# Reordering the small steps around a fused MLP stage: factors, weight halves, row loads and low parts moved

## The chip, the cores and the metric

The kernel runs on one core of a Trainium2 chip. The core has five instruction streams that matter here: PE (matrix products, 128x128), DVE (elementwise and reductions, reads PSUM), ACT (elementwise with a function table, reads PSUM), POOL (elementwise, SBUF only) and SP, which in this kernel only issues DMA transfers. Each stream executes in its own program order; streams wait for each other through semaphores. The metric is the device time of one execution in microseconds (us), the median of several runs.

## The reference

The input x is a sequence of 2048 rows of 448 numbers, in float32. Two branches and a skip are added:

```python
xn = layernorm(x)                       # eps 1e-5, no scale or shift
q = xn @ wq                             # 16 heads of 28
k, v = xn @ wk, xn @ wv                 # one shared key and value head of 28
o = softmax(q k^T * 28**-0.5) v         # per head, over all 2048 keys
y = layernorm(xn)                       # the second norm of the MLP branch
h = gelu(y @ w1 + b1)                   # 448 -> 1792, tanh form
out = x + o @ wo + (h @ w2 + b2)        # 1792 -> 448
```

## The kernel before, in words

Rows are handled in four chunks of 512 (`NCH`, 4 tiles of 128 each, `CT`). There is no planner: `tc.manual_schedule()` keeps the order in which the Python code emits instructions, engine by engine, and the framework only adds the waits. So a step that stands earlier in the code stands earlier on its engine, and an engine whose next instruction waits holds everything behind it. All DMA of this part goes through SP's queue, in code order.

Products are made in three parts for accuracy: a value is split into a rounded high part and a low part (the rest), and high*high, low*high and high*low are accumulated.

Stage 1, the projections (about the first 66 us). For each chunk c and each of four column groups i, `q_slot` emits eleven products into one PSUM bank. The eviction of a group (`evac`) is emitted one slot later: for chunks 2 and 3 DVE multiplies the bank by a row of factors (L388), ACT rounds it to the high part (L389), and `low()` lets DVE subtract for the low part (L396) and issues the stores of both parts to DRAM (`qd`, L403) and, for group 0, the key rows (`ks`, L399). Between these, `w1_split` cuts the first MLP weight into parts (ACT L353, POOL L354, L355), and a dictionary `more` places small jobs at slots by `later(c, i, job)`. Among those jobs are the norm factors. `bn_end` turns means and variances into the factors of the first norm by `rstd` (DVE L200, ACT square root L202, DVE L203 to L206, and the shift, L246). Chunk 0 needs a second set of factors for the second norm; it is made in two generators of two tiles each, at slots (2,2) and (2,3), followed by a Tanh on one element that makes ACT load the table used from then on (L448).

Stage 2, the MLP (about 66 to 471 us). It is a row of 56 slots, `slot(n)`, one for each chunk and each 128-wide block of the 1792 hidden columns, in the chunk order 2, 3, 0, 1, plus two more to drain. A slot n emits `mlp1`, the eleven products of block n, then two ACT reads of the bank (hx L643, hz L644) and two POOL steps (L645, L646); then it emits `mlp2` of block n-2, twelve products (L673) of the finished hidden block with `w2` into four banks. In between, by a table `stages` whose key is the product's number, stand: `texp` (two exponentials L613 and, behind the second, four stores of 256 KB to DRAM, `td`, L616), `closing` (ACT rounds the previous block, hh L656; POOL makes its low part, hl L658) and `middle` (ACT tanh L649, POOL L650, L651). A block therefore passes hx, hz, L645, L646, tanh, L650, L651, hh, hl before its `mlp2` two slots later. The second weight is cut two blocks at a time by `w2_split`: `high` on ACT (L367), `low` half on DVE and half on POOL (L371), then the load of a further pair (L359). In the first slots of chunk 2 there is a special order, `n == 1` and `n == 2`. The memory of `w2h` and `w2l` is that of the projections' tiles, so their first writes wait for the last stores of the projections.

Two other jobs fill each slot, one step behind every few products: `mxs`, the row maximum of query-key products for the softmax (PE L561, DVE L562), of which 784 are spread over the MLP and attention stages, and `tq`, whole rows of scores of some heads kept transposed later (PE L595, DVE L596 into `raw`, two buffers, a buffer being free again when its `td` stores have landed). Both take PSUM banks `m` from a ring of three.

For each chunk's result the rows of x are loaded again (`line`, L271, 224 KB each, tile `a` with four buffers) from block 10 on, and POOL adds b2 one block later (L728, L731). The last `mlp2` of a chunk adds the bank to them (DVE L678) and stores them (`ad`, L679). At block 8 of the last chunk `load_q(0)` clears a tile on POOL (L524) and issues four query loads on SP (L530).

Stage 3, attention (about 471 us to the end), is not touched. It takes as many of the `mxs` steps in each of its steps as its weights give it of those that are left, so that what the MLP stage does not do is done there.

Of the kernel before, what the change touches and what calls it, by code (L numbers as in the profile page):

```python
# [16 lines left out]
P = 128  # L17
# [24 lines left out]
def block_kernel(ctx, tc, x, wq, wk, wv, wo, w1, b1, w2, b2, out):  # L42
# [150 lines left out]

    def rstd(dst, var, n, norms):
        m = len(norms)
        v = tmp.tile([P, 3, m, n], F32, name=f"rs{m}{n}", bufs=2)
        s, r, w = (v[:, i] for i in range(3))
        for i, second in enumerate(norms):
            by, plus = (1.0 + EPS, EPS * EPS) if second else (1.0, EPS)
            dve.tensor_scalar(s[:, i], var, by, plus, op0=ALU.mult, op1=ALU.add)  # L200
        yield s
        act.activation(r, s, AF.Sqrt)  # L202
        dve.reciprocal(r, r)  # L203
        dve.scalar_tensor_tensor(w, r, -0.5, r, op0=ALU.mult, op1=ALU.mult)
        dve.tensor_mul(w, w, s)
        dve.scalar_tensor_tensor(dst, w, 1.5, r, op0=ALU.add, op1=ALU.mult)  # L206
        yield
# [9 lines left out]
    def bn_end(c, k0=0, n=CT):  # L217
        for k in range(k0, k0 + n):
            dve.bn_aggr(lnp[:, CT * c + k, :], sts[c][:, k, :])
        ts = slice(CT * c + k0, CT * c + k0 + n)  # L220
        norms = (False, True) if c else (False,)
        r = rstd(lnrq[:, 0:len(norms), ts], lnp[:, ts, 1], n, norms)
        at = next(r)
        yield
        next(r)
        shift(c in KEPT, ts)
        yield
        if c in KEPT:
            ratio = ratios[c] = tmp.tile([P, CT], F32, name="ratio", bufs=2)
            dve.tensor_mul(ratio, at[:, 1], lnq[:, ts])  # L230
            dve.tensor_mul(ratio, ratio, lnr[:, ts])
        elif c:
            shift(True, ts)
        else:
            r = rstd(lnrq[:, 1:2, ts], lnp[:, ts, 1], n, (True,))
            next(r)
            yield
            next(r)
            shift(True, ts)
        yield  # L240

    ratios = {}
# [14 lines left out]
    def stats(c):  # L257
        for k in range(CT):
            bn(CT * c + k)
        g = bn_end(c)  # L260
        next(g)
        next(g)
        return g
# [38 lines left out]

    def norm_first(bank):
        center, turn = norm_parts(0, False, True, bank)
        ends = seconds
        bn(0)
        bn(1)
        next(ends[0])
        next(ends[0])
        bn(2)  # L310
        bn(3)
        next(ends[1])
        center(0)
        center(1)
        next(ends[1])
        spin(21)
        turn(0)
        spin(2)
        turn(1)
        center(2)  # L320
        center(3)
        spin(8)
        turn(2)
        spin(1)
        turn(3)
        next(first)
# [98 lines left out]
            pe.matmul(idle if t is None else t, ident, ident, start=True, stop=True)  # L425

    idle = mtile([P, P])
    seconds = [bn_end(0, 0, 2), bn_end(0, 2, 2)]
    norm_first(qbank)
    seconds.append(stats(1))  # L430
    more = {}

    def later(c, i, job, ahead=False):
# [2 lines left out]
    for c, at in ((2, ((0, 1), (0, 2), (0, 2), (0, 3))), (3, ((1, 0), (1, 1), (1, 2), (1, 3)))):  # L436
# [4 lines left out]
            later(c - 1, 0, lambda g=g: next(g), True)  # L441
        later(c - 1, 1, lambda g=g: next(g))
        later(c - 1 if c == 2 else c, 3 if c == 2 else 0, lambda c=c: unscale(c), c == 3)
    for g, at in zip((seconds[0], seconds[1], seconds[2]), ((2, 2), (2, 2), (1, 0))):
        later(*at, lambda g=g: next(g))
    for g in seconds[0:2]:
        later(2, 3, lambda g=g: next(g))
    later(2, 3, lambda: act.activation(warm, one, AF.Tanh))  # L448

    def b1_turn():  # L450
        pb = mtile([P, NF])
# [25 lines left out]
    for c in range(NCH):  # L477
        if c + 1 < NCH:
            center, turn = norm_parts(c + 1, False, bank=lambda shape: (qbank, mtile)[next(turns) % 2](shape))
        for i in range(4):  # L480
            ev = q_slot(c, i)
            if vt is not None:
                v_slot(c, vt)
                vt = None
            low = None
            if evac is not None:
                vt, low = evac()
            evac = ev
            if i in ((2, 3) if c == 0 else (1, 3)):
                n = 2 * c + i // 3  # L490
                w1_split(n)
                if n < 2:
                    w1_load(n + 4)
                elif n == 3:
                    w1_load2(6)
                elif n in (4, 5):
                    w2_load(n - 4)
                if n in (2, 3):
                    qms.append(load_m(*heads[n - 2]))
                elif n in (4, 5):  # L500
                    load_m(TURNED[n - 4], 3, q3[n - 4])
            for job in more.get((c, i, True), ()):
                job()
            for part, k in (("", "c0 c1", "t0 c2 t1 c3", "t2 t3") if c == 0 else
                            ("c0 c1", "t0 c2 t1 c3", "t2 t3", "") if c + 1 < NCH else [""] * 4)[i].split():
                if part == "t" and low is not None:
                    low()
                    low = None
                (center if part == "c" else turn)(int(k))
            if low is not None:  # L510
                low()
            for job in more.get((c, i, False), ()):
                job()
    evac()[1]()
    for c in KEPT:
        xts[c, True] = xts.pop((c, False))
    ph1a.close()
# [115 lines left out]
    def split(c, ft):  # L633
        return c == 0 and ft % 2 == 1

    def mlp1(c, ft):
        yh, yl = xts[MLP_ORDER[c], True]
        ph = m2p.tile([P, CW], F32, name="m2_3") if (c, ft) == (0, 1) else php.tile([P, CW], F32, name="ph")
        fs = slice(ft * P, (ft + 1) * P)
        yield from proj_steps(ph, lambda b: w1h[:, b, fs], lambda b: w1l[:, b, fs], yh, yl)  # L640
        hx = hrp.tile([P, CW], F32, name="hx", bufs=2)
        hz = hrp.tile([P, CW], F32, name="hz", bufs=2)
        act.activation(hx, ph, AF.Identity, bias=b1t[:, ft:ft + 1])  # L643
        act.activation(hz, ph, AF.Square, bias=b1s[:, ft:ft + 1], scale=GELU[0] ** 0.5)  # L644
        pool.tensor_scalar(hz, hz, 1.0, 1.0, op0=ALU.mult, op1=ALU.add)  # L645
        pool.tensor_mul(hz, hz, hx)  # L646

        def middle():
            act.activation(hz, hz, AF.Tanh, scale=GELU[1])  # L649
            pool.tensor_scalar(hz, hz, 0.5, 0.5, op0=ALU.mult, op1=ALU.add)  # L650
            pool.tensor_mul(hx, hx, hz)  # L651

        def ending():
            hh = hrp.tile([P, CW], F32R, name="hh")
            hl = hrp.tile([P, CW], F32R, name="hl")
            act.activation(hh, hx, AF.Copy)  # L656
            hs[c, ft] = (hh, hl)
            pool.tensor_sub(hl, hx, f(hh))  # L658

        return middle, ending  # L660

    def mlp2(c, ft, stages):
        if ft == 0:
            m2s[c] = [m2p.tile([P, CW], F32, name=f"m2_{k}")[:, 0:D] for k in range(CT)]
        m2 = m2s[c]
        hh, hl = hs.pop((c, ft))
        terms = ((hh, w2h), (hh, w2l), (hl, w2h))
        order = [(k, i) for k in range(CT) for i in range(3)]
        if (c, ft) == (0, 0):
            order.sort(key=lambda e: e[1])  # L670
        for n, (k, i) in enumerate(order):
            h, w = terms[i]
            pe.matmul(m2[k], h[:, k * P:(k + 1) * P], w[:, ft, :], start=(ft == 0 and i == 0),  # L673
                      stop=(ft == NF - 1 and i == 2))
            if ft == NF - 1 and i == 2:
                t = CT * MLP_ORDER[c] + k
                a = lines.pop(t)
                dve.tensor_add(a, a, m2[k])  # L678
                nc.sync.dma_start(ad[:, t, :], a)  # L679
            stages[n]()  # L680
            yield

    def slot(n):
# [1 line left out]
        middle = high = low = none  # L685
        closing, ending = ending, none
        if n < len(mslots):
            if split(*mslots[n]):
                high, low = w2_split(n // 2)
                if n > 1:  # L690
                    high()
            middle, ending = yield from mlp1(*mslots[n])
        if n == 2:
            for _ in range(3):
                maxed += mxs.step()
            later_low()
        texp = turned_exp if n < len(mslots) - 1 else none
        stages = {0: texp, 1: texp, 2: low, 3: closing, 5: middle}
        if n == 1:
            stages, later_low = {0: closing, 1: high, 5: middle}, low  # L700
        if n in norms:
            stages = {4: norms[n], 5: texp, 6: texp, 7: closing, 8: norms[n], 9: middle, 10: low}
        if n >= 2:
# [16 lines left out]
    for n in range(len(mslots) + 2):  # L720
        c, ft = mslots[n] if n < len(mslots) else (NCH, n - len(mslots))
        if 3 <= ft < 11 and ft % 2 and len(KEPT) <= c + 1 < NCH:
            line(CT * MLP_ORDER[c + 1] + (ft - 3) // 2)
        if 9 < ft:
            line(CT * MLP_ORDER[c] + ft - 10)
            if ft > 10:
                a = lines[CT * MLP_ORDER[c] + ft - 11]
                pool.tensor_add(a, a, b2b)  # L728
        if ft == 0 and n:
            a = lines[CT * MLP_ORDER[c - 1] + CT - 1]  # L730
            pool.tensor_add(a, a, b2b)  # L731
        if (c, ft) == (NCH - 1, 8):
# [281 lines left out]
```

## Time and profile before

| what | value |
|---|---|
| median of three runs | 1086.64 us (1086.4 to 1087.1) |
| the profiled execution | 1086.84 us |
| its span, first to last instruction | 1085.1 us |
| around the span | 1.7 us |
| granted clock of PE | 0.999 |
| PE busy | 1072.9 us, 5889 products |
| DVE, ACT, POOL busy | 907.4, 726.8, 562.0 us |

A row of the timeline has: start in us from the span's beginning, length, engine, line of the kernel, operation, output<-inputs, shape, and in brackets how long that engine had been idle before it and what ended the idle time. SPq is SP issuing DMA. Rows of equal instructions are merged (x4). A row of the windows has: the stretch, its length, busy us and instruction count of PE, PEld (weight loads), DVE, ACT, POOL, then the granted clock, the mean busy share of the DMA engines and their GB/s. The product instructions overlap by about half, so starts, not lengths, tell PE's pace.

### The profile page before, as it was taken

Reading aid. Unit: us, or ns where it says so; the run is one execution under the profiler, and the core shown is the slowest. Engines: PE = TensorE matmul, PEld = TensorE weight load, DVE = VectorE, ACT = ScalarE, POOL = GpSimd, SP = SyncE. Lnnn points to the kernel's source line nnn. Section 1 sums busy time; section 2 is a strip of 40 time slices with the busy share of each in tenths; the row PEclk is TensorE's granted clock in tenths of the full one; section 3 lists DMA queues with packets and bytes.
Section 4 is the critical chain, followed back from the end, with each engine's and each line's share of the span. In section 5 each row is a group of like instructions: output and inputs, shape, how many; then the busy total and the mean of one; then the engine's idle time right before and its main releaser. Section 6 shows DMA issues by size and latency. Waiting matters only on the chain.

```text
span 1085.1 us, 17677 instructions
## 1 busy us (share of the span) xinstructions
PE 1072.9 (99%) x5889; PEld 721.6 (67%) x5889; DVE 907.4 (84%) x1846; ACT 726.8 (67%) x1262; POOL 562.0 (52%) x694
## 2 busy tenths in 40 slices
PE   9989999999999999999999999999999999999998
PEld 8768888888888888865555556555556555555455
DVE  6789899898988998877999997899997889886744
ACT  6665556666666666559777776677775777765784
POOL 5359897778777877854333433433442343243220
PEclk9999999999999999999999999999999999999999
DMA  8774456777877777776977798588796778885820
GB/s 268 251 213 140 121 142 170 195 179 179 214 187 180 184 196 192 210 163 152 201 187 185 179 219 206 145 196 190 184 212 172 177 174 199 201 200 131 186 53 34
DMA packets 140102, 194.45 MB, mean 179 GB/s; under 512 B 17078, under 2 KB 95596, under 8 KB 140012
## 3 DMA queue, kind: packets, MB, share of 16 engines
q1 hardware_dynamic: 127276, 171.43, 62.8%
q0 software_dynamic: 11328, 21.33, 8.5%
q8 instruction: 46, 0.75, 0.3%
q10 hardware_dynamic: 1408, 0.57, 0.2%
q14 instruction: 44, 0.36, 0.1%
HBM read 114.30 MB, written 77.71 MB: 177 GB/s over the span
## 4 chain that ended last, share of the span: by engine, by line
PE 90%; DMA 4%; DVE 3%; issue 1%; POOL 1%; ACT 1%; SPq 0%; DVEq 0%; POOLq 0%; ACTq 0%
PE po L903 21%; PE m L561 18%; PE m L931 17%; PE m L673 12%; PE ph L182 10%; PE m L595 5%; DMA raw<-in_B_w_dram 1%; PE m L793 1%; PE m L794 1%; PE m L795 1%; PE ph L185 1%; PE ph L187 1%; PE po L886 1%; PE m L886 1%; DMA a<-in_A_x_dram 1%
## 5 line engine op out<-in xcount | busy, mean ns | idle before, releaser
L562 DVE TENSOR_REDUCE mx<-m 128x1 f32<-128x512 f32 x784 | 506.5, 679 | 78.2 <-PE m L561 68.4
L932 ACT ACTIVATE p<-m 128x512 f32<-128x512 f32 x784 | 402.6, 609 | 161.4 <-PE m L931 161.2
L561 PE MATMUL m<-ks,qm 128*128 128x512 f32 x784 | 321.4, 410 | 0.7 <-DVE mx L562 0.6
L931 PE MATMUL m<-xh,ks 128*128 128x512 f32 x784 | 257.3, 397 | 0.1
L903 PE MATMUL po<-p,vs 128*32 128x512 f32 x1920 | 230.8, 598 | 0.0
L561 PEld LDWEIGHTS m<-ks,qm 128*128 128x128 f32 x784 | 147.0, 187 | 116.8 <-ACT p L932 37.0
L596 DVE TENSOR_SCALAR_CACHE_REDUCE raw<-m 128x512 f32<-128x512 f32 x240 | 161.6, 689 | 17.4 <-PE m L595 10.6
L931 PEld LDWEIGHTS m<-xh,ks 128*128 128x128 f32 x784 | 146.1, 188 | 42.1 <-issue 5.8
L914 DVE STREAM_TRANSPOSE p<-half 128x1024 f32<-128x1024 f32 x120 | 148.2, 1236 | 5.3 <-PE m L886 2.0
L613 ACT ACTIVATE raw<-raw,m 128x1024 f32<-128x1024 f32 x120 | 133.0, 1150 | 2.0 <-DVE m L602 2.0
L903 PEld LDWEIGHTS po<-p,vs 128*32 128x32 f32 x1920 | 50.1, 109 | 113.4 <-issue 108.4
L643 ACT ACTIVATE hx<-ph,b1t 128x512 f32<-128x512 f32 x55 | 37.9, 690 | 124.2 <-PE ph L187 120.2
L595 PE MATMUL m<-ks,q 128*128 128x512 f32 x240 | 94.6, 394 | 1.7 <-DVE raw L596 1.7
L658 POOL TENSOR_TENSOR hl<-hx,hh 128x512 fp32r<-128x512 f32 x56 | 72.5, 1295 | 33.2 <-ACT hh L656 33.2
L673 PE MATMUL m<-w2h,hl 128*128 128x448 f32 x224 | 82.1, 368 | 1.4 <-POOL hl L658 1.4
L673 PE MATMUL m<-w2l,hh 128*128 128x448 f32 x224 | 81.4, 365 | 0.6 <-DVE w2l L371 0.6
L673 PE MATMUL m<-w2h,hh 128*128 128x448 f32 x224 | 81.3, 364 | 0.2 <-DMA td<-raw 0.2
L646 POOL TENSOR_TENSOR hz<-hz,hx 128x512 f32<-128x512 f32 x56 | 72.8, 1300 | 4.7
L548 POOL DMA_DIRECT2D xh<-mn x15 | 8.2, 545 | 129.2 <-ACT mn L544 129.2
L651 POOL TENSOR_TENSOR hx<-hx,hz 128x512 f32<-128x512 f32 x56 | 72.4, 1293 | 4.7
L182 PE MATMUL ph<-xh,w1h 128*128 128x512 f32 x165 | 65.0, 394 | 0.0
L182 PE MATMUL ph<-xh,w1l 128*128 128x512 f32 x165 | 64.5, 391 | 0.0
(182 smaller groups left out, 1384.0 us busy)
## 6 DMA issues: line engine op xcount, KB each, us to landing
td<-raw SPq DMA_DIRECT2D x240, 256.0 KB
half<-td SPq DMA_DIRECT2D x120, 512.0 KB
xh<-qd POOLq DMA_DIRECT2D x60, 168.0 KB, 4.2
a<-in_A_x_dram SPq DMA_DIRECT2D x28, 224.0 KB
qm<-qd POOLq DMA_DIRECT2D x112, 56.0 KB, 4.2
qd<-qe SPq DMA_DIRECT2D x24, 256.0 KB
qm<-qd SPq DMA_DIRECT2D x84, 56.0 KB
ad<-a SPq DMA_DIRECT2D x16, 224.0 KB
```

The costliest lines, as they stand in the source:

```text
L182: pe.matmul(ps, w, v, start=(n == 0), stop=False)
L561: pe.matmul(pm, qm[:, t * P:(t + 1) * P], ks[:, n * CW:(n + 1) * CW], start=True, stop=True)
L562: dve.tensor_reduce(mx[:, CT * j + t, n:n + 1], pm, axis=AX.X, op=ALU.max)
L595: pe.matmul(sc, q3[i][:, t * P:(t + 1) * P], ks[:, n * CW:(n + 1) * CW], start=True, stop=True)
L596: dve.tensor_scalar(raw[:, :, 4 * n:4 * n + 4, :].rearrange("p r b i -> p b r i"), sc.rearrange("p (b r i) -> p b r i", r=4, i=32), SCALE, ...
L613: act.activation(raw[:, rs], raw[:, rs], AF.Exp, bias=m3[:, 4:5], scale=1.0)
L646: pool.tensor_mul(hz, hz, hx)
L673: pe.matmul(m2[k], h[:, k * P:(k + 1) * P], w[:, ft, :], start=(ft == 0 and i == 0), stop=(ft == NF - 1 and i == 2))
L903: pe.matmul(po[32 * j:32 * j + 32, :], vs[:, kt, :], ps.pop((u, kt, j)), start=(kt == 0), stop=(kt == NT - 1))
L914: dve.transpose(p.rearrange("p k (g j) -> p g k j", j=32), halves[u, kt // 8][:, :, 32 * (kt % 8):32 * (kt % 8) + 64].rearrange("p g (k j) ...
L931: pe.matmul(s, ks[:, kt * P:(kt + 1) * P], qss[u][:, j, :], start=True, stop=True)
L932: act.activation(p, s, AF.Exp, scale=SCALE)
```

## The change

The four parts of the change are these.

1. The second factors of chunk 0 are made for all four tiles in one generator, `second_of_first`, at slots (3,0) and (3,1), and the Tanh that loads the table follows at (3,1). `rstd` keeps one buffer instead of two where it works on four tiles; `ratio` has three instead of two.
2. In slot (3,3) of the projections the eviction of (3,3), its product with the factors and its rounding, is emitted at once, ahead of the low part of (3,2).
3. In the first three MLP slots: `w2_split(0)` and its `high` stand at the end of slot 0, its `low` in slot 1; `middle` stands earlier in slots 0 and 1; three `mxs` steps that slot 2 took ahead of its `mlp2` are left out there.
4. In the last chunk the rows of x are loaded at blocks 5 to 8 and b2 added at blocks 6 to 9. In the last slot `closing` of block 12 stands ahead of the two ACT reads of block 13. In the very last `mlp2` the twelve products go by pairs of banks: hh with w2h for both, hh with w2l for both, then hl with w2h for both.

```diff
     def rstd(dst, var, n, norms):
-        v = tmp.tile([P, 3, m, n], F32, name=f"rs{m}{n}", bufs=2)
+        v = tmp.tile([P, 3, m, n], F32, name=f"rs{m}{n}", bufs=2 if n < CT else 1)
...
-        else:
-            r = rstd(lnrq[:, 1:2, ts], lnp[:, ts, 1], n, (True,))
-            next(r)
-            yield
-            next(r)
-            shift(True, ts)
+        yield
+
+    def second_of_first():
+        ts = slice(0, CT)
+        r = rstd(lnrq[:, 1:2, ts], lnp[:, ts, 1], CT, (True,))
+        next(r)
+        yield
+        next(r)
+        shift(True, ts)
         yield
...
-    for g, at in zip((seconds[0], seconds[1], seconds[2]), ((2, 2), (2, 2), (1, 0))):
-        later(*at, lambda g=g: next(g))
-    for g in seconds[0:2]:
-        later(2, 3, lambda g=g: next(g))
-    later(2, 3, lambda: act.activation(warm, one, AF.Tanh))
+    later(1, 0, later_one)
+    g = second_of_first()
+    for k in (0, 1):
+        later(3, k, lambda g=g: next(g))
+    later(3, 1, lambda: act.activation(warm, one, AF.Tanh))
...
                 (center if part == "c" else turn)(int(k))
+            if (c, i) == (NCH - 1, 3):
+                _, end = evac()
             if low is not None:
                 low()
...
-    evac()[1]()
+    end()
...
     def mlp1(c, ft, before):
...
+        before()
         act.activation(hx, ph, AF.Identity, bias=b1t[:, ft:ft + 1])
...
             order.sort(key=lambda e: e[1])
+        if (c, ft) == (NCH - 1, NF - 1):
+            order.sort(key=lambda e: (e[0] // 2, e[1]))
...
-            if split(*mslots[n]):
+            if split(*mslots[n]) and n > 1:
                 high, low = w2_split(n // 2)
-                if n > 1:
-                    high()
-            middle, ending = yield from mlp1(*mslots[n])
-        if n == 2:
-            for _ in range(3):
-                maxed += mxs.step()
-            later_low()
+                high()
+            before = none
+            if n == len(mslots) - 1:
+                before, closing = closing, none
+            middle, ending = yield from mlp1(*mslots[n], before)
         texp = turned_exp if n < len(mslots) - 1 else none
         stages = {0: texp, 1: texp, 2: low, 3: closing, 5: middle}
+        if n == 0:
+            high, later_low = w2_split(0)
+            stages = {0: texp, 1: middle, 2: texp, 3: high}
         if n == 1:
-            stages, later_low = {0: closing, 1: high, 5: middle}, low
+            stages = {0: closing, 1: later_low, 2: middle}
...
-        if 9 < ft:
-            line(CT * MLP_ORDER[c] + ft - 10)
-            if ft > 10:
-                a = lines[CT * MLP_ORDER[c] + ft - 11]
-                pool.tensor_add(a, a, b2b)
-        if ft == 0 and n:
+        k = ft - (10 if c < NCH - 1 else 5)
+        if c < NCH and 0 <= k < CT:
+            line(CT * MLP_ORDER[c] + k)
+        if c < NCH and 0 < k <= CT:
+            a = lines[CT * MLP_ORDER[c] + k - 1]
+            pool.tensor_add(a, a, b2b)
+        if ft == 0 and 0 < c < NCH:
```

More of the change, by code (lines that the diff above doesn't have):

```diff
@@ L228, in bn_end @@
         if c in KEPT:
-            ratio = ratios[c] = tmp.tile([P, CT], F32, name="ratio", bufs=2)
+            ratio = ratios[c] = tmp.tile([P, CT], F32, name="ratio", bufs=3)
             dve.tensor_mul(ratio, at[:, 1], lnq[:, ts])
@@ L304, in norm_first @@
         center, turn = norm_parts(0, False, True, bank)
-        ends = seconds
+        ends = [bn_end(0, 0, 2), bn_end(0, 2, 2)]
         bn(0)
@@ L427, in block_kernel @@
     idle = mtile([P, P])
-    seconds = [bn_end(0, 0, 2), bn_end(0, 2, 2)]
     norm_first(qbank)
-    seconds.append(stats(1))
+    g = stats(1)
+    later_one = lambda g=g: next(g)
     more = {}
@@ L634, in split, with mlp1 @@
         return c == 0 and ft % 2 == 1
-    def mlp1(c, ft):
+    def mlp1(c, ft, before):
         yh, yl = xts[MLP_ORDER[c], True]
```

## The prediction

> **What bounds the kernel now.** I read first the busy shares, then the groups of instructions with their idle time, then the windows, and last the timeline of PE around the places that the change touches. The two rows below are of the page: the share of PE, and what the last products of a hidden block wait for.
>
> ```profile
> PE 1072.9 (99%) x5889; PEld 721.6 (67%) x5889; DVE 907.4 (84%) x1846; ACT 726.8 (67%) x1262; POOL 562.0 (52%) x694
> L673 PE MATMUL m<-w2h,hl 128*128 128x448 f32 x224 | 82.1, 368 | 1.4 <-POOL hl L658 1.4
> ```
>
> The windows show (PE, PEld, DVE, ACT, POOL, then clock, DMA share, GB/s) that the clock is full and that nothing is left to gain in the attention stage:
>
> ```profile
> 480.00:1060.00 580.00, 580.00 (x3480) 310.50 (x3473) 477.03 (x875) 419.42 (x810) 209.27 (x336) 1.00 0.76 178
> ```
>
> PE is the bound throughout: 580.00 of 580 us there, 1072.9 in all. The number of products stays what it was, so only an idle gap of PE can be closed or opened. Those within reach of the change are in the timeline (the bracket is PE's idle time and who ended it):
>
> ```profile
> 62.47 0.43 PE L410 MATMUL m<-ident,vt 32*128 32x32 f32 x4 [0.69 <-ACT vt L393]
> 70.11 0.50 PE L595 MATMUL m<-ks,q 128*128 128x512 f32 x1 [1.33 <-DVE raw L596]
> ...
> 78.53 0.44 PE L673 MATMUL m<-w2h,hh 128*128 128x448 f32 x1 [0.23 <-DMA td<-raw]
> 80.67 0.67 PE L673 MATMUL m<-w2l,hh 128*128 128x448 f32 x2 [0.61 <-DVE w2l L371]
> 87.11 0.37 PE L673 MATMUL m<-w2h,hl 128*128 128x448 f32 x1
> ...
> 436.86 0.50 PE L595 MATMUL m<-ks,q 128*128 128x512 f32 x1 [0.40 <-DVE raw L596]
> 463.77 0.47 PE L673 MATMUL m<-w2h,hl 128*128 128x448 f32 x1 [0.74 <-POOL hl L658]
> 468.09 0.47 PE L673 MATMUL m<-w2h,hl 128*128 128x448 f32 x1 [0.69 <-POOL hl L658]
> 472.13 0.50 PE L561 MATMUL m<-ks,qm 128*128 128x512 f32 x1 [0.58 <-DVE mx L562]
> ```
>
> Early 0.69+1.33+0.23+0.61 = 2.86, in the last MLP chunk 0.40, at its end 0.74+0.69+0.58 = 2.01: 5.27 us, 0.49% of the time. That is all that the change could win. The sum is made against the profiled execution (1086.84 us, span 1085.1 and 1.7 around it), 0.20 above the median of 1086.64.
>
> **Part 1 and 2, the projections' end.** DVE and POOL at slot (2,3), then ACT and DVE at the end of (3,3):
>
> ```profile
> 55.43 1.44 DVE L204 SCALAR_TENSOR_TENSOR rs<-rs 128x2 f32<-128x2 f32 x1
> 57.09 0.52 DVE L206 SCALAR_TENSOR_TENSOR lnrq<-rs 128x2 f32<-128x2 f32 x1
> 58.58 0.69 DVE L388 TENSOR_TENSOR qp<-qp,ib 128x512 f32<-128x512 f32 x1
> ...
> 55.24 1.61 POOL L354 TENSOR_TENSOR w1l<-raw,w1h 128x672 fp32r<-128x672 f32 x1 [6.24 <-issue]
> 55.31 1.28 ACT L448 ACT_TABLE_LOAD   x1
> 66.62 0.94 ACT L353 ACTIVATE w1h<-pair 128x896 fp32r<-128x896 f32 x1
> 68.14 0.60 ACT L389 ACTIVATE qe<-qp 128x512 fp32r<-128x512 f32 x1 [0.57 <-ACT w1h L353]
> 67.36 0.69 DVE L388 TENSOR_TENSOR qp<-qp,ib 128x512 f32<-128x512 f32 x1
> 69.37 0.68 DVE L596 TENSOR_SCALAR_CACHE_REDUCE raw<-m 128x512 f32<-128x512 f32 x1
> ```
>
> The factor chain is eleven small DVE steps from 55.2 to 58.6. Two of them (1.44 and 0.52, where their likes in the second chain take 0.16) lie beside POOL's L354: DVE is held. So the bank of (2,3), at 58.58, is multiplied some 3.4 us after its turn. The change takes both chains out here: that multiply comes at about 54.8, and the 0.69 at 62.47 goes (its vt is a job of ACT that stood behind the late banks). One chain of six steps comes back at (3,0) and (3,1), behind another w1 split. POOL's steps of that split stand beside it again, so I charge it the same 1.44+0.52+3x0.16 = 2.4, and the table load of 1.28 falls on ACT before a rounding. One square root fewer on ACT costs less than 0.3 and hides beside PE. The last multiply (67.36) comes to about 65.7: the low part of (3,2) no longer stands ahead of it, 0.7 from the order, and 1.0 from the gap closed before. ACT then does the last split (66.62 moves little) and the rounding at 67.1 to 67.6 rather than 68.14. DVE's last low part ends, and the first raw eviction starts, at about 68.4 rather than 69.37. The fourth L595 stands at 69.1 rather than 70.11: **a lead of 1.0 us**. Bounds: none of it, if the rounding stays behind the split and the chain is held for longer; 1.33, the whole gap.
>
> **Part 3, w2 and the first slots.** Does the lead reach mlp2? Rows of SP, the windows of 72 to 75, DVE, PE and POOL:
>
> ```profile
> 66.54 4.68 SPq L403 DMA_DIRECT2D qd<-qe  x8
> ...
> 72.00:73.00 1.00, 1.00 (x6) 0.79 (x5) 1.00 (x3) 0.88 (x1) 0.26 (x1) 1.00 1.01 369
> 73.00:74.00 1.00, 1.00 (x6) 0.84 (x5) 1.00 (x3) 1.00 (x2) 0.00 (x0) 1.00 0.21 72
> 74.00:75.00 1.00, 1.00 (x6) 0.84 (x5) 1.00 (x2) 1.00 (x3) 0.08 (x1) 1.00 0.00 0
> ...
> 74.56 0.69 DVE L596 TENSOR_SCALAR_CACHE_REDUCE raw<-m 128x512 f32<-128x512 f32 x1
> 79.65 0.96 DVE L371 TENSOR_TENSOR w2l<-raw,w2h 128x448 fp32r<-128x448 f32 x1
> 70.92 0.40 PE L561 MATMUL m<-ks,qm 128*128 128x512 f32 x1
> 71.16 0.39 PE L182 MATMUL m<-xh,w1l 128*128 128x512 f32 x1
> ...
> 76.88:86.82 9.94, 9.10 (x40) 7.09 (x39) 9.40 (x18) 7.44 (x10) 9.69 (x11) 1.00 0.34 82
> ```
>
> w2's memory is free when the last query stores have landed. DMA is full until 73 and empty from 74, so the first high half can start at about 74.2. It takes 0.94 (its like is 66.62). Put at the end of slot 0 it stands on ACT ahead of hx(1) and hz(1), and DVE's low half (0.96) ahead of the four raw evictions that began at 74.56. So these begin at 75.1+0.96 = 76.1, and the fourth L595 waits for a bank; I charge 0.4 us of new idle. The gaps of 0.23 and 0.61 at 78.53 and 80.67 have their cause removed. The first mlp2 starts at about 77.7 rather than 78.53, but 3 x 0.24 = 0.7 us of that (an L561 to the next product, 70.92 to 71.16) is the three products that now run in the attention stage, where PE has no gap to take them.
>
> The next gate is POOL. The last window is from the start of L645(1) to the end of hl(1): POOL is busy 9.69 of 9.94 us, so hl(1) comes when that row of steps is through. L645(1) needs hx(1) and hz(1), which stand behind the high half: 74.2+0.94, then two reads of some 0.7 each, so it begins at about 76.5 rather than 76.88, and 9.6 us later hl(1) ends at about 86.1 rather than 86.82. PE uses hl(1) at 87.11 before and at about 86.06 after: 1.05 gained, less 0.7 = **0.35**. Parts 1 to 3 together win 0.4. SP: the next w2 load goes out a slot sooner, into DMA that is empty at 74 to 75, at no cost; if it met the stores of `td` instead, they would land later by its share. Bounds: if part 3 only stalls, 0.9 lost; if both gaps close and the lead stays, 1.0 gained.
>
> **Part 4a, the rows of the last chunk.** POOL and SP around block 8, and the gap that follows:
>
> ```profile
> 423.28 1.81 POOL L524 MEMSET xh<- 128x2048 f32 x1
> 425.11 1.65 SPq L530 DMA_DIRECT2D xh<-qd  x4
> 426.87 3.58 SPq L616 DMA_DIRECT2D td<-raw  x4
> 429.00:430.00 1.00, 1.00 (x6) 0.81 (x6) 0.99 (x3) 0.00 (x0) 0.92 (x1) 1.00 0.99 213
> 435.00:436.00 1.00, 1.00 (x6) 0.83 (x5) 0.00 (x0) 0.00 (x0) 1.00 (x2) 1.00 0.54 172
> 436.10 0.69 DVE L596 TENSOR_SCALAR_CACHE_REDUCE raw<-m 128x512 f32<-128x512 f32 x1 [1.87 <-PE m L595]
> 459.23 1.15 POOL L728 TENSOR_TENSOR a<-a,b2b 128x448 f32<-128x448 f32 x1
> ```
>
> Four loads and four adds move; three of the four adds fall on idle POOL. The add of block 8 takes 1.15 and now stands right before the memset of 423.28. SP's four query loads wait for the memset (425.11 = 423.28+1.81), and behind them in SP's order stand the four `td` stores of 426.87. DVE's eviction at 436.10 is ready 1.87 us before it runs, DMA being 0.99 busy at 429: it waits for those stores to free a `raw` buffer, and PE's 0.40 at 436.86 is what is left of that wait. So the add goes through whole: memset 424.4, loads 426.3, stores 428.0, eviction 437.25, PE idle 0.40+1.15 = 1.55. **Loss 1.15.** Bounds: a gain of 0.40, if the store's issue isn't what the eviction waits for; a loss of 2.3 if a row load also stands in front (a rival, below). I take the add alone, as the memset and the issues follow each other without a gap.
>
> **Part 4b, the end of the MLP.** POOL and PE:
>
> ```profile
> 462.43 1.29 POOL L658 TENSOR_TENSOR hl<-hx,hh 128x512 fp32r<-128x512 f32 x1
> 466.77 1.27 POOL L658 TENSOR_TENSOR hl<-hx,hh 128x512 fp32r<-128x512 f32 x1
> 471.16 0.40 PE L931 MATMUL m<-xh,ks 128*128 128x512 f32 x1
> ```
>
> `closing` of block 12 comes two ACT reads sooner: hl(12) ends at about 461.3 rather than 463.72, and the 0.74 at 463.77 goes. POOL's chain of block 13 starts behind it and ends at the same 468.02, so what PE gains there it waits at hh(13) and hl(13). By pairs of banks, eight L673 and three L561 are left behind hl(13), where there were ten and four: the 3.07 us from 468.09 to 471.16 for fourteen products become 3.07x11/14 = 2.4, and the attention's L931 starts at 470.5. The last adds on DVE move with it, and so does the 0.58 at 472.13. **Gain 0.6.** Bounds: 0, if the last three adds crowd DVE and the maximum comes later; 1.4, if the 0.69 at 468.09 shrinks as well.
>
> **Sum:** 1086.84 - 0.4 + 1.15 - 0.6 = 1087.0, and 0.2 less for the median: 1086.8 us.
>
> **The rivals.** (A) Faster: the wait at 436.10 is a wait for transfers in flight, not for their issue, so the add costs nothing; and parts 1 to 3 keep all of the lead and both w2 gaps: 1.0+0.23+0.61+0.11. With 0.6 to 1.1 at the end this is 2.5 to 3.0, hence about 1084. For it speaks that DMA is only 0.54 busy just before the eviction; against it, that DVE is then idle and a store whose issue is late lands late.
>
> (B) Slower in 4a: SP's row load of slot 50 is issued ahead of the query loads and the stores. Its 224 KB at the 213 GB/s of the window at 429 are 1.1 us more, so the gap grows to 2.65 and the time is 1087.9. The window's share of 0.99 speaks for it; against it, that the load can go out while SP waits for the memset. The Trainium skill, page "DMA: Bandwidth & Descriptors", section "Queues, rings and completion order", has a rule for it: on each DMA engine descriptors are consumed in the order of the ring, so what is issued first is read first. By that rule the row load is always in front, and the sum would be 1087.9 rather than 1086.8; no row here shows the order within a ring.
>
> (C) The other side, clearly slower: the new place of w2's first high half turns the landing of the last query store into a gate for everything. ACT waits with hx(1) behind it, DVE with the four evictions behind w2's low half. Each us that the landing is past 74.2 then costs one. It decides from 76.2, where 2 us are lost and the end is 1089. For it: the last eight stores are issued only from 66.54 to 71.2. Against it: DMA carries 72 GB/s at 73 and nothing at 74.
>
> (D) The change moves gaps and closes none: the three products cost 0.7 and give 0.7, hl(13) is as late as before, and the time is 1086.6.
>
> **How the numbers follow.** My forecast has a chance of 0.50, A 0.16, B 0.17, C 0.12, D 0.05. About 0.2% (2.2 us) is what a measurement of this kernel can tell from no change. Faster by more than that (below 1084.5) is most of A: 0.15. Slower by more (above 1088.8) is C and a part of B where further loads add up: 0.17. Within it is the rest, 0.68. Range: from 1084.4, A's value with a little lost, to 1089.0, C's point of decision. The likeliest case alone, by its bounds, reaches from 1085.2 to 1088.2.
>
> **What would show it.** Part 1: the multiply of (2,3) at 55 rather than 58.58, no idle at 62.47, the idle before the fourth L595 about as long but 1 us sooner. Part 3: w2's first high half on ACT at 74 to 75, hl(1) ending by 86.1. Part 4a: POOL's memset at 424.4 and PE idle for 1.5 at the eviction after block 8; if it stays under 0.5 the step is wrong. Part 4b: the idle of 0.74 gone and L931 at 0.6 sooner against the gap before it. Most of all a chain of small DVE steps in chunk 3 held longer than 2.4 us would make the prediction wrong, or a POOL step that is late for another reason.

## The result and the profile after

The changed kernel takes 1088.51 us (median of 11 runs, 1087.24 to 1090.46) beside 1086.78 for the kernel before on the same chip (1085.93 to 1087.67): 1.0019 of it, 95% interval 1.0011 to 1.0027. It is slower by 1.7 us, where 0.2 was forecast; the time lies in the range, and the cause was not the one in the sum. A second series of the same kernel (below) gave 1088.13. The mean granted clock is 0.997 or 0.998 in six of the eleven executions, which are the six longest (1088.51 to 1090.46), and 0.999 or 1.000 in the other five (1087.24 to 1088.44).

Lines below 200 are the same in both kernels; behind that the changed kernel's are 3 to 10 higher (L595 is now L600, L596 L601, L561 L566, L673 L681, L371 L374, L367 L370, L651 L657 and L645 L651). The timeline of the changed kernel, PE's longer idle times first, then ACT, DVE and POOL:

```profile
70.16 0.47 PE L600 MATMUL m<-ks,q 128*128 128x512 f32 x1 [2.56 <-DMA ks<-qe]
78.71 0.50 PE L600 MATMUL m<-ks,q 128*128 128x512 f32 x1 [0.32 <-DVE raw L601]
88.17 0.47 PE L681 MATMUL m<-w2h,hl 128*128 128x448 f32 x1 [0.65 <-POOL hl L664]
438.60 0.50 PE L600 MATMUL m<-ks,q 128*128 128x512 f32 x1 [1.29 <-DVE raw L601]
468.45 0.47 PE L681 MATMUL m<-w2h,hh 128*128 128x448 f32 x1 [0.72 <-ACT hh L662]
1046.54 0.42 PE L896 MATMUL m<-p,vs 128*32 128x256 f32 x4 [0.58 <-ACT p L942]
...
76.38 0.95 ACT L370 ACTIVATE w2h<-raw 128x896 fp32r<-128x896 f32 x1 [2.07 <-DMA qd<-qe]
54.35 0.69 DVE L391 TENSOR_TENSOR qp<-qp,ib 128x512 f32<-128x512 f32 x1
59.65 1.40 DVE L204 SCALAR_TENSOR_TENSOR rs<-rs 128x4 f32<-128x4 f32 x1
61.28 0.51 DVE L206 SCALAR_TENSOR_TENSOR lnrq<-rs 128x4 f32<-128x4 f32 x1
424.12 1.16 POOL L738 TENSOR_TENSOR a<-a,b2b 128x448 f32<-128x448 f32 x1
425.22 1.81 POOL L529 MEMSET xh<- 128x2048 f32 x1
```

The multiply of (2,3) is at 54.35 (forecast 54.8), and the 0.69 at 62.47 is gone. But PE meets a new wait of 2.56 for the key rows (`ks`), so that the fourth L600 stands at 70.16, no sooner than before (70.11). w2's first high half waits 2.07 us on ACT for the last query stores. The windows of the same kernel (the granted clock stands behind POOL's column) show what the long wait did:

```profile
72.00:73.00 1.00, 1.00 (x4) 0.81 (x3) 0.16 (x1) 1.00 (x2) 0.00 (x0) 0.50 1.06 399
73.00:74.00 1.00, 1.00 (x3) 0.79 (x3) 0.69 (x1) 1.00 (x2) 0.62 (x1) 0.50 1.08 402
```

PE runs at half clock there: three or four products in a microsecond, where the kernel before had six. The profiled execution took 1089.34 us, 0.8 over its median, and is one of the six with a clock under 0.999, so a second profile is needed.

### The profile page after: what moved, and what is told of

It is laid out like the page before. It is cut to its first block, busy times and chain, and to the rows that moved or that the text cites. A ratio compares the mean times of both kernels' runs of the same rounds, so it can differ in the third digit from the quotient of the medians.

```text
span 1087.6 us, 17656 instructions
## 1 busy us (share of the span) xinstructions
PE 1074.0 (99%) x5889; PEld 722.3 (66%) x5889; DVE 906.3 (83%) x1840; ACT 726.8 (67%) x1261; POOL 560.5 (52%) x694
## 4 chain that ended last, share of the span: by engine, by line
PE 91%; DVE 3%; DMA 2%; POOL 1%; ACT 1%; issue 1%; SPq 0%; DVEq 0%; ACTq 0%; POOLq 0%
PE po L913 20%; PE m L566 18%; PE m L941 17%; PE m L681 12%; PE ph L182 9%; PE m L600 5%; PE m L803 1%; PE m L804 1%; PE m L805 1%; PE ph L185 1%; PE ph L187 1%; DMA td<-raw 1%; PE m L428 1%; PE qp L182 1%; PE po L896 1%; PE m L896 1%
## 5 line engine op out<-in xcount | busy, mean ns | idle before, releaser
L566 PE MATMUL m<-ks,qm 128*128 128x512 f32 x784 | 321.7, 410 | 0.1
L566 PEld LDWEIGHTS m<-ks,qm 128*128 128x128 f32 x784 | 147.3, 188 | 114.8 <-ACT p L942 41.6
L601 DVE TENSOR_SCALAR_CACHE_REDUCE raw<-m 128x512 f32<-128x512 f32 x240 | 161.5, 690 | 19.5 <-PE m L600 9.7
L600 PE MATMUL m<-ks,q 128*128 128x512 f32 x240 | 94.8, 395 | 4.2 <-DMA ks<-qe 2.6
L681 PE MATMUL m<-w2h,hl 128*128 128x448 f32 x224 | 81.8, 368 | 0.7 <-POOL hl L664 0.6
L681 PE MATMUL m<-w2h,hh 128*128 128x448 f32 x224 | 81.0, 364 | 0.7 <-ACT hh L662 0.7
L681 PE MATMUL m<-w2l,hh 128*128 128x448 f32 x224 | 81.3, 364 | 0.0
L657 POOL TENSOR_TENSOR hx<-hx,hz 128x512 f32<-128x512 f32 x56 | 72.5, 1295 | 4.7
L472 POOL DMA_DIRECT2D qm<-qd x112 | 57.3, 519 | 28.4 <-PE m L941 25.8
L535 POOL DMA_DIRECT2D xh<-qd x60 | 38.2, 637 | 56.6 <-PE m L566 49.6
```

What stands on the lines that cost most here:

```text
L566: pe.matmul(pm, qm[:, t * P:(t + 1) * P], ks[:, n * CW:(n + 1) * CW], start=True, stop=True)
L600: pe.matmul(sc, q3[i][:, t * P:(t + 1) * P], ks[:, n * CW:(n + 1) * CW], start=True, stop=True)
L601: dve.tensor_scalar(raw[:, :, 4 * n:4 * n + 4, :].rearrange("p r b i -> p b r i"), sc.rearrange("p (b r i) -> p b r i", r=4, i=32), SCALE, ...
```

## The experiments

Each kernel ran 11 times beside the kernel before (1086.70, 1086.80 and 1086.69 in the three series).

**The changed kernel again.** No edit. This run is told first because its profile is the one that the readings below rest on; it was among the last to run.

> The changed kernel once more, for a second profile. If the wait of 2.56 us for the key rows and the granted clock of 0.5 behind it are a regular part of it, they are there again. If they are of one execution in which SP's queue ran late from the start (its query stores of the first chunks were already 1.2 us late), the wait before the fourth score product is 1.3 us or less, the clock stays 1.00, the second wait, at 77 to 78 us, is 1.2 to 2.0 us instead, and the median is 1088.5 all the same.

1088.13 us; the profiled execution took 1088.00. Its timeline, PE first, then ACT, DVE and POOL:

```profile
68.61 0.47 PE L600 MATMUL m<-ks,q 128*128 128x512 f32 x1 [0.81 <-DVE raw L601]
77.10 0.50 PE L600 MATMUL m<-ks,q 128*128 128x512 f32 x1 [1.85 <-DVE raw L601]
77.90 0.36 PE L681 MATMUL m<-w2h,hh 128*128 128x448 f32 x1
86.56 0.47 PE L681 MATMUL m<-w2h,hl 128*128 128x448 f32 x1 [0.66 <-POOL hl L664]
437.23 0.50 PE L600 MATMUL m<-ks,q 128*128 128x512 f32 x1 [1.07 <-DVE raw L601]
467.11 0.48 PE L681 MATMUL m<-w2h,hh 128*128 128x448 f32 x1 [0.73 <-ACT hh L662]
...
74.77 0.95 ACT L370 ACTIVATE w2h<-raw 128x896 fp32r<-128x896 f32 x1 [1.62 <-DMA qd<-qe]
75.81 0.62 DVE L374 TENSOR_TENSOR w2l<-raw,w2h 128x448 fp32r<-128x448 f32 x1 [2.78 <-ACT w2h L370]
76.35 0.68 DVE L601 TENSOR_SCALAR_CACHE_REDUCE raw<-m 128x512 f32<-128x512 f32 x1
76.96 0.62 POOL L651 TENSOR_SCALAR hz<-hz 128x512 f32<-128x512 f32 x1 [2.77 <-ACT hz L650]
```

So the long wait is not in every execution. In the first profile SP's queue was 1.6 us later: it issued the key rows from 65.20 and the last query stores from 68.58, here from 63.64 and 67.02, and the stores let ACT go on at 76.38, here at 74.77. The shift is 1.55 at the fourth product, ahead of the half clock, and 1.61 behind it (first use of the low part of block 1, `hl(1)`, at 88.17 and 86.56), so the half clock is hidden in the wait for the stores. It is not one execution alone, though: the clock was under 0.999 in six of the eleven of the first series and in one of this one. Without these seven the median of the two series is 1088.0, so some 1.3 us of the loss have another cause.

The picture at full clock is this one: the fourth product is 1.5 us sooner than before (68.61 for 70.11), and then PE loses 1.85 us at the next fourth product, because DVE stands with w2's low half (idle 2.78), which waits for ACT's high half (idle 1.62), which waits for the query stores. The lead is not 1.5 in every profile. The nine that have parts 1 and 2, without the late one, have the fourth product at 68.28 to 70.04, with a median of 69.04; the four without them at 69.85 to 70.11. The lead is about 1.0.

**Part 3 taken back.**

```diff
...
+        if n == 2:
+            for _ in range(3):
+                maxed += mxs.step()
+            later_low()
...
-        if n == 0:
-            high, later_low = w2_split(0)
-            stages = {0: texp, 1: middle, 2: texp, 3: high}
         if n == 1:
-            stages = {0: closing, 1: later_low, 2: middle}
+            stages, later_low = {0: closing, 1: high, 5: middle}, low
```

> The changed kernel with part 3 taken back (w2's first high half in slot 1, its low half in slot 2, middle and the three maximum products where they were); parts 1, 2 and 4 stay. Theory W: w2's first high half, at 76.38 in the changed kernel, no longer stands ahead of the two reads of block 1; those come 2 us sooner, the row of steps on POOL ends sooner, and the time falls by 1 to 1.8 us to about 1087. Theory S: the wait of 2.56 us for the key rows and the low clock behind it stay, and the time falls by under 0.7 us.

1086.24 us, 0.9998 of before (0.9989 to 1.0007): 2.3 less than the changed kernel (1.9 less than its second series). Part 3 costs more than the whole loss. That is more than theory W asked for, and the wait that theory S meant is 0.66 us in its profile.

**Parts 1 and 2 taken back.**

```diff
...
-    g = second_of_first()
-    for k in (0, 1):
-        later(3, k, lambda g=g: next(g))
-    later(3, 1, lambda: act.activation(warm, one, AF.Tanh))
...
+    for g in seconds[0:2]:
+        later(2, 3, lambda g=g: next(g))
+    later(2, 3, lambda: act.activation(warm, one, AF.Tanh))
...
-            if (c, i) == (NCH - 1, 3):
-                _, end = evac()
...
-    end()
+    evac()[1]()
```

> The changed kernel with parts 1 and 2 taken back (the two short factor chains at slots (2,2) and (2,3), no early eviction in slot (3,3)); parts 3 and 4 stay. Theory S (the stores and key rows on SP's queue gate the end of the projections; PE, now early, waits 2.56 us for the key rows and its granted clock falls to 0.5 for some 3.5 us after it): the wait before the fourth score product is back at about 1.3 us, the clock stays at 1.00 there, and 1.5 to 2.5 us of the 1.7 lost come back: about 1086.5 us. Rival W (only part 3 hurts: w2's first high half waits for the last stores): the time stays within 0.5 us of the changed kernel's 1088.5, or grows, since the lead is gone.

1087.88 us, 1.0012 (1.0004 to 1.0021): far from the 1086.5 of theory S, and 0.6 below the 1088.5 of W, which allowed 0.5. The gap of 1.33 is back (at 70.03), and still only some 0.2 to 0.6 us separate it from the changed kernel's two series, which the scatter hardly tells from nothing. In this company the lead of parts 1 and 2 is worth nothing.

**Each alone.** The kernel before with parts 1 and 2 alone, and with part 3 alone (the edits are the reverse of those above).

> The kernel before with parts 1 and 2 alone. Theory G (part 3 puts the landing of the last query stores in the way and so eats the lead that parts 1 and 2 make): without part 3 the lead reaches the attention stage; the gaps of PE up to 90 us add up to 1.2 less than before, and the time is 1085.4 to 1085.8. Rival N (the lead is worth nothing because SP's queue and the key rows are as late as before): 1086.4 to 1086.9.

> The kernel before with part 3 alone. Theory G: without a lead to eat, part 3 costs less than the 2.3 us that it costs in the changed kernel: by u12_factors_back, where it stands without parts 1 and 2 but with part 4, some 0.8 us are left: 1087.3 to 1087.7. Rival F (part 3 has a fixed price): 1086.7+2.3 = 1089.0.

Parts 1 and 2 alone: 1085.64 us, 0.9990 (0.9981 to 0.9999), 1.05 faster. Part 3 alone: 1087.73 us, 1.0009 (1.0000 to 1.0018), 1.04 slower. In the changed kernel part 3 costs 1.9 to 2.3, an excess of about 1, the lead of parts 1 and 2. Theory G came out in both times. Its gaps did not: up to 90 us they add up to 0.7 less than before, not 1.2, but the one profile of parts 1 and 2 alone is of an execution of 1086.61, 1.0 over its median, with the fourth product at 70.04.

What the lead meets can be read from POOL, at the start of block 1's first step (L645, L651 in the changed kernel). With w2 in its old place it starts at 76.62 and 76.88 without parts 1 and 2, and at 74.98 to 76.24 in the four profiles with them. With part 3 it starts at 77.62 and 77.77 without them, and at 76.96 to 78.57 in the six with them. Part 3 alone has these rows (the same step is L646 there):

```profile
75.43 0.95 ACT L367 ACTIVATE w2h<-raw 128x896 fp32r<-128x896 f32 x1 [0.65 <-ACT raw L613]
77.62 0.62 POOL L646 TENSOR_SCALAR hz<-hz 128x512 f32<-128x512 f32 x1 [1.80 <-ACT hz L645]
77.76 0.50 PE L595 MATMUL m<-ks,q 128*128 128x512 f32 x1 [1.05 <-DVE raw L596]
```

So behind part 3 the lead no longer shows. PE's wait is 1.05 and 1.24 without the lead, and 1.85 to 1.96 with it, wherever DVE's low half stands in front and the clock is full.

**Part 3 and the rows taken back**, which leaves parts 1, 2 and 4b. The edit is the one of part 3 above, with the lines of the rows as before.

> The changed kernel with part 3 and part 4a taken back; parts 1, 2 and 4b stay. If the costs of the two parts are separate (2.3 us for part 3 by u3_w2_back, 0.8 for the rows by u4a_rows_back) they add: 1088.5-2.3-0.8 = 1085.4 us, some 1.3 below the kernel before. If they overlap, the time stays at 1086.2.

1085.53 us, 0.9987 (0.9978 to 0.9996): the costs add, and this version beats both kernels. Its profiled execution (1084.93) is 0.6 below its median. Its timeline:

```profile
68.28 0.47 PE L600 MATMUL m<-ks,q 128*128 128x512 f32 x1 [0.72 <-DVE raw L601]
76.62 0.44 PE L681 MATMUL m<-w2h,hh 128*128 128x448 f32 x1 [0.21 <-DMA td<-raw]
78.75 0.47 PE L681 MATMUL m<-w2l,hh 128*128 128x448 f32 x1 [0.61 <-DVE w2l L374]
85.20 0.37 PE L681 MATMUL m<-w2h,hl 128*128 128x448 f32 x1
434.82 0.50 PE L600 MATMUL m<-ks,q 128*128 128x512 f32 x1 [0.23 <-DVE raw L601]
...
72.84 0.67 ACT L649 ACTIVATE hx<-m,b1t 128x512 f32<-128x512 f32 x1
75.59 0.93 ACT L370 ACTIVATE w2h<-raw 128x896 fp32r<-128x896 f32 x1
72.66 0.69 DVE L601 TENSOR_SCALAR_CACHE_REDUCE raw<-m 128x512 f32<-128x512 f32 x1
74.98 0.62 POOL L651 TENSOR_SCALAR hz<-hz 128x512 f32<-128x512 f32 x1
```

This is what part 3 displaced. With w2 in its old place ACT reads block 1 at 72.84, ahead of the high half at 75.59, and POOL starts that block's L651 at 74.98; with part 3 these are behind it (the second profile of the changed kernel), and POOL starts at 76.96. DVE's raw evictions are at 72.66 rather than 76.35. PE's first use of hl(1) is at 85.20 rather than 86.56, although three more products stand ahead of it.

**Is it DVE's place or ACT's?** The changed kernel, with DVE's low half in slot 2:

```diff
-            stages = {0: closing, 1: later_low, 2: middle}
+            stages = {0: closing, 2: middle}
...
+        if n == 2:
+            later_low()
```

> The changed kernel with DVE's half of w2's first low part in slot 2, as before, and ACT's high part still at the end of slot 0. If DVE, waiting with w2's low part, is what holds the four raw evictions and with them PE (gaps of 1.2 to 2.0 us at 77 to 78), that gap falls under 0.3. If the block's reads on ACT behind the high part set the end all the same, the wait at the low part of block 1 (0.65) grows by what the other lost, and the time stays within 0.4 of 1088.5; if DVE alone is the cause the time falls by 1.2 or more, to 1087.3.

1088.23 us: no change. Its PE, ACT and DVE:

```profile
78.01 0.47 PE L681 MATMUL m<-w2h,hh 128*128 128x448 f32 x1 [1.57 <-ACT hh L662]
87.29 0.47 PE L681 MATMUL m<-w2h,hl 128*128 128x448 f32 x1 [0.63 <-POOL hl L664]
...
75.33 0.95 ACT L370 ACTIVATE w2h<-raw 128x896 fp32r<-128x896 f32 x1 [2.04 <-DMA qd<-qe]
77.33 0.62 ACT L662 ACTIVATE hh<-hx 128x512 fp32r<-128x512 f32 x1
73.53 0.69 DVE L601 TENSOR_SCALAR_CACHE_REDUCE raw<-m 128x512 f32<-128x512 f32 x1
```

DVE's evictions are free at 73.53, and the idle 1.85 at 77.10 has gone, but PE waits 1.57 for `hh`, which stands on ACT behind the same high half. The wait for hl(1) did not grow (0.63), against that half of the expectation. So ACT's order, the high half ahead of the block's reads and rounding, is enough to hold the time; DVE's place is a second wait, about as long, beside it. Whether DVE's place alone would cost as much is not shown, nor what `middle` and the second exponential do in their new places, which no run moved alone.

**The three products kept in slot 2.**

```diff
+        if n == 2:
+            for _ in range(3):
+                maxed += mxs.step()
```

> The changed kernel with the three maximum products kept in slot 2 ahead of its mlp2 (w2's places as changed). The runs with part 3 all show a gap of 0.58 us of PE near 1046 and 0.3 us more after PE's last product, the runs without it do not. If the three products that are moved into the attention stage cause these, both go, and the three products fill 0.65 us of the wait for the low part of block 1: the time falls by about 0.9 us, to 1087.6. If they belong to w2's new place, they stay, and the time stays at 1088.5 or above.

1088.53 us, no gain. The windows of 1000 to 1060, first of the changed kernel's second profile, then of this one:

```profile
1000.00:1060.00 60.00, 59.42 (x426) 30.78 (x428) 36.49 (x61) 46.66 (x93) 12.57 (x17) 1.00 0.54 120
```

```profile
1000.00:1060.00 60.00, 60.00 (x418) 31.55 (x421) 37.54 (x64) 46.71 (x93) 12.61 (x17) 1.00 0.51 120
```

The idle 0.58 near 1046 is in all seven profiles that have part 3 without these products, and in none of the others, so they cause it. So do the 0.3 us more behind PE's last product. Both went and the median stayed. The profile shows what took it back. PE's weight loads of the second and third product wait for DVE's late raw evictions, which hold the banks that these products need:

```profile
78.97 0.19 PEld L566 LDWEIGHTS m<-ks,qm 128*128 128x128 f32 x1 [0.42 <-DVE raw L601]
79.58 0.19 PEld L566 LDWEIGHTS m<-ks,qm 128*128 128x128 f32 x1 [0.43 <-DVE raw L601]
```

The wait for hl(1) has gone, but its first use stands 12.54 us behind the start of w2's high half, where the changed kernel's second profile has 11.79: 0.75 lost for the 0.9 won later. The medians compare poorly here besides, as seven of the eleven executions had a clock of 0.998.

**The rows taken back, and the add behind the memset.** First the changed kernel with the rows at their old blocks; then, with part 3 taken back, the rows at blocks 5 to 8 but the add emitted behind the query loads:

```diff
+        if (c, ft) == (NCH - 1, 8):
+            load_q(0)
         if c < NCH and 0 < k <= CT:
             a = lines[CT * MLP_ORDER[c] + k - 1]
             pool.tensor_add(a, a, b2b)
...
-        if (c, ft) == (NCH - 1, 8):
-            load_q(0)
```

> The changed kernel with the rows of the last chunk loaded at blocks 10 to 13 again and b2 added at 11 to 14; all else stays. If the add ahead of the memset is the cause of the gap of 1.29 us at 438.6, the gap falls back to about 0.4 and the time falls by 0.9 us, to 1087.6. If the row loads in the ring cost more than the gap shows, it falls by 1.5 or more. If the gap is one of run to run differences, it stays at about 1.3 and the time at 1088.5.

> The changed kernel with part 3 taken back and the rows still loaded at blocks 5 to 8, but with the add of block 8 behind the memset and the query loads instead of ahead of them. If the add's place on POOL ahead of the memset is the whole cost of part 4a, the gap of about 1.2 us after block 8 falls to 0.4 or less and the time is that of v1_no_w2_no_rows, 1085.4. If the row load ahead of the stores in SP's queue costs it, the gap stays near 1.2 and the time at 1086.2.

Rows back: 1087.75 us, 0.8 less than the changed kernel's first series and 0.4 less than its second. Add behind: 1085.70 us, 0.9988 (0.9979 to 0.9997), beside 1086.24 with the add in front and 1085.53 without the move; the intervals of the three overlap. PE's gap after block 8 in the runs with rows back, with the add in front (part 3 taken back) and with the add behind, one fence each:

```profile
436.71 0.50 PE L600 MATMUL m<-ks,q 128*128 128x512 f32 x1 [0.18 <-DVE raw L601]
```

```profile
436.50 0.50 PE L600 MATMUL m<-ks,q 128*128 128x512 f32 x1 [1.19 <-DVE raw L601]
```

```profile
422.20 1.80 POOL L529 MEMSET xh<- 128x2048 f32 x1
423.96 1.16 POOL L742 TENSOR_TENSOR a<-a,b2b 128x448 f32<-128x448 f32 x1
435.95 0.50 PE L600 MATMUL m<-ks,q 128*128 128x512 f32 x1 [0.56 <-DVE raw L601]
```

Between 0.18 and 1.19 lies the add; put behind the memset it gives back 0.63 of that, with the row loads where the change put them. The gap did not fall to the 0.4 that was expected; whether the last 0.3 are the row load's is not shown.

**The end of the MLP.** Part 4b taken back from the changed kernel, and alone on the kernel before:

```diff
-        if (c, ft) == (NCH - 1, NF - 1):
-            order.sort(key=lambda e: (e[0] // 2, e[1]))
...
-            if n == len(mslots) - 1:
-                before, closing = closing, none
```

> The changed kernel with the last slot's rounding of block 12 behind the two reads of block 13 again, and the last twelve products bank by bank; all else stays. The gaps of 0.74, 0.69 and 0.58 at the end of the MLP come back in place of the 0.72: the time grows by 0.6 to 1.3 us, to 1089.1 to 1089.8. If part 4b wins nothing it stays at 1088.5.

> The kernel before with part 4b alone: the gaps of 0.74, 0.69 and 0.58 at the end of the MLP become 0.73+0.10+0.15 as in the other runs with it: the time falls by 0.4 to 1.0 us, to 1085.7 to 1086.3. If the wait only moves, by as much as the pair order and the sooner low part win at first, it stays at 1086.7.

Taken back: 1088.64 us, a difference of 0.1 to 0.5, where 0.6 to 1.3 was expected. Alone: 1086.54, 1.0000 of before (0.9991 to 1.0009), where 0.4 to 1.0 less was expected. The gaps there, alone:

```profile
466.62 0.47 PE L676 MATMUL m<-w2h,hh 128*128 128x448 f32 x1 [1.06 <-ACT hh L657]
468.29 0.47 PE L676 MATMUL m<-w2h,hl 128*128 128x448 f32 x1 [0.36 <-POOL hl L659]
...
471.86 0.51 PE L937 MATMUL m<-xh,ks 128*128 128x512 f32 x1 [0.15 <-ACT p L938]
```

0.74+0.69+0.58 = 2.01 became 1.06+0.36+0.15 = 1.57: 0.4 gained by the gaps, too little for the times to show. In the changed kernel it is 0.72 or 0.73 and at most 0.15 more, as the adds of the rows no longer stand on POOL there: the rows give back at the end some 0.6 us of what they cost at block 8.

## Why the prediction was right or wrong

The range held, the size did not: 1.4 to 1.7 us slower for 0.2. That the time lies in the range is owed to its upper bound, which was rival C's; the sum itself had one part with the wrong sign.

- **Parts 1 and 2: right.** Step by step: 54.35 for 54.8; DVE held for 1.40 and 0.51, charged as 1.44 and 0.52 (the second of the two lies beside POOL's L355, not L354 as the prediction has it); the fourth product 1.0 us sooner in the median of the profiles, as forecast. Alone they give 1.05 us.
- **Part 3: the failed step.** The single times were close: high half 74.77 (74.2), raw evictions 76.35 (76.1), POOL's first step of block 1 at 76.96 (76.5), the row of nine POOL steps to hl(1)'s end 9.5 us (9.6), use of hl(1) 86.56 (86.06, which is 0.04 before the end of hl(1) that the prediction itself gives). The sum was wrong in what it compared them with. "I charge 0.4 us of new idle" was too small even without the lead, where the wait is 1.05 to 1.24, and with the lead it is 1.85 to 1.96. And "it begins at about 76.5 rather than 76.88" was held against the kernel before, not against the 74.98 to 76.24 that it has with parts 1 and 2 and w2 in its old place. So "Parts 1 to 3 together win 0.4" stands against a loss of about 1 us (1.05 won, 1.9 to 2.3 lost). It was rival C's mechanism, named at 0.12: the landing of the last query stores as a gate. C counted each us past 74.2 as a loss and reached a total like the measured one only at 76.2. With the lead, ACT could read block 1 at 72.84, so the count starts sooner than C had it; no run moved the landing to show from where.
- **The three products** were charged 0.7 us of PE time with no idle. They also open 0.58 of idle near 1046 and 0.3 at the end, which no step foresaw. Put back, they wait 0.85 for banks, so leaving them out neither won nor lost.
- **Part 4a: right in mechanism, too large in size.** The add goes through whole to the memset, and the gap rises from 0.40 or less without it to 1.02 to 1.33 with it (forecast 1.55). The medians say 0.4 to 0.8 for 1.15, as part of it comes back at the end. Rival B's 1.1 us did not come: with the row load still ahead in SP's queue the time is within 0.2 us of that without. The Trainium skill, page "DMA: Bandwidth & Descriptors", section "Queues, rings and completion order", has the descriptors of a ring consumed in order; of a cost from it, the gap's last 0.3 us are all that these runs leave room for.
- **Part 4b: too large.** 0.6 forecast; 0.1 to 0.5 measured, and alone no gain clear of the noise. "What PE gains there it waits at hh(13) and hl(13)" held: 1.06 and 0.36 there for 0.74 and 0.69 before, so only the last gap, 0.58 to 0.15, gave anything.
- **The other rivals.** D fell: gaps close in parts 1 and 2 and open in part 3, and the two are not equal. A fell with part 3 and the add. Its lead, without part 3, is what the best version has; w2's gaps of 0.21 and 0.61 stay there.

## What to carry to other kernels

When two edits stand in the same chain, price the second against the chain as the first leaves it: a lead ahead of a fixed gate is worth nothing, and the stall at the gate grows with the lead. An instruction that waits for a transfer must not be put ahead of work that is ready on its queue; look at what stands behind it on that engine, not at the engine's idle time. Before a long instruction of an idle-looking engine is moved, see which queue waits for the one behind it.

## What the runs showed of the hardware

In one profile an idle of 2.56 us of PE was followed by a granted clock of 0.62, 0.50, 0.50 and 0.67 in the four microseconds from 71 to 75; it fell at 71.25, 1.1 us after PE had begun again. Idles of 1.85 (the second profile) and up to 1.96 in other runs were not followed by a lower clock. The Trainium skill, page "TensorE: Matmul & The Clock Gate", section "Part 1: The HAM clock gate", gives about 3.4 us of idle for that; here 2.56 was enough.

A mean clock of 0.997 or 0.998 came in 21 of 66 executions of the changed kernel and its variants that keep the lead and w2's new place together, in one of 66 of those that keep only one of the two, and in one of 99 of the kernel before. So it comes mostly where the two stand together. Only one of these executions has a profile; which wait lowered the clock in the others is not shown.

DVE's small steps of 0.16 us took 1.40 and 0.51 beside POOL's w1 split in its new place, and 1.44 and 0.52 in the old. Each ends within 0.02 us of the POOL step beside it (before: 56.87 and 56.85, 57.61 and 57.60), so it is the neighbour, not the number of columns (2 or 4), that sets it.
